# A second fold of the Fourier transform, along the sequence and along the channels, in an attention and Fourier-mix kernel

## The chip, the cores and the metric

The kernel runs on one core of one Trainium2 chip. The core has a matrix engine (TensorE, "PE" in the profile, with its weight loads as "PEld"), three engines for elementwise work (VectorE "DVE", ScalarE "ACT", GpSimd "POOL"), and a queue engine (SyncE, "SP") that here only issues DMAs. Matrix products land in PSUM[...]. The metric is the device time of one execution in microseconds (us). Every measurement is of the whole program.

## The reference

The program is talking-heads attention followed by an FNet block. Cut to what matters:

```python
# q, k, v: (8, 12, 448, 64); w_pre, w_post: (12, 12); all float32
scores = scale * (q @ k.transpose(0, 1, 3, 2))
scores = einsum('bhij,hg->bgij', scores, w_pre)       # mix the heads before softmax
attn = exp(scores - max(scores)); attn = attn / (sum(attn) + 1e-09)
attn = einsum('bhij,hg->bgij', attn, w_post)          # mix the heads after softmax
x = (attn @ v) as (8, 448, 768)                       # heads side by side
mixed = real(fft(fft(x, axis=1), axis=2))             # along 448 rows, then along 768 columns
u = x + mixed
un = (u - mean(u)) / sqrt(var(u) + 1e-06)
out = u + relu(un @ w_ch1) @ w_ch2                    # 768 -> 3072 -> 768
```

The Fourier transform is computed as products with tables of cosines and sines: the real part is a cosine product in both directions minus a sine product in both directions.

## The kernel before

Two phases follow each other. The **mix phase** (`mix_phase`) does attention and the Fourier transform for 8 batches; the **feed-forward phase** (`ffn_phase`) does the norm and the two big products. The change is in the first, apart from how the second reads its rows from DRAM.

**Steps of the mix phase.** A batch has 24 steps; there are 192 of them. One step T handles a set of query rows for all heads. Its chain runs over the engines: `emit_gather` (SyncE) brings scores of all heads together into `Kr`; `emit_premix` (TensorE, L425) mixes heads into the PSUM tile `mx`, of which there is one; `emit_max` (VectorE, L433) takes the row maximum; `emit_exp` (ScalarE, L441) writes the exponentials to `PP` and their sums to `den`; `emit_scale` makes the reciprocal on VectorE (L449, L450) and multiplies `PP` by it on **GpSimd** (L452, two instructions); `emit_postmix` (TensorE, L462) mixes heads again into `po`; `emit_turn` (VectorE, L473) transposes 32x32 blocks into `Pv`. The scaling of step T is emitted in loop step T-2 (`LM = 2`), its second mix in loop step T. So a loop step s holds the first mix of step s+2, then the second mix of step s, and then whatever is due.

**What is due** in a loop step comes from tables of step numbers: `AT_T` (transposes of q and k, L376), `AT_QK` (the score products, L399), `AT_AV` (products with v, L489), `AT_X` (transposes of the result to rows of x, L525), `AT_Z` (first stage of the Fourier transform, L570) and `AT_S` (its second stage, L584). Numbers above 24 reach into the steps of the next batch. On TensorE, VectorE and ScalarE the order of the program is the order in which these functions are called. On GpSimd and SyncE the framework's scheduler places the instructions[...].

**The rows and the folds.** The 448 rows of a batch are held as four groups `gi` of 112 or 113 rows (`X`): groups 1 and 3 are stored backward, so that row s of one tile meets row 448-s of the other. `fold` (GpSimd) is called when group 1 or 3 has been transposed. It makes, for the pair of groups, the sum and the difference of the two tiles (L547, two halves each), and from each the sum or difference of column d and column 768-d: `xe` (L551, L552) has 385 columns and `xo` (L557) 383. These six closures are put into the list `folds`, of which the loop takes one per step. In the queue of GpSimd they stand one behind the other: in a stretch of the queue that belongs to one batch the scheduler put all six between two scalings, once for the pair 0 and 1 and once for the pair 2 and 3.

**The two stages.** `emit_z` multiplies `xe` or `xo` (as the weights) with a table `ts` of 225 columns, for chunks of 96 to 128 columns of x: four chunks for the even part, three for the odd, each with two products, one per pair of groups, which accumulate. `emit_s2` multiplies the evacuated `z` with the tables `tce` or `tdo` of 385 columns: for each of two pairs four products for the even part and three for the odd. Its evacuation `done` adds the result to x in place on VectorE (L595, L597), and after the odd part sends the rows to the DRAM tensor of the batch, `u_scr[b]`: forward rows by DMAs from SyncE (L610, L612), backward rows by an indirect DMA from GpSimd (L604), which scatters them by a list of row numbers. The feed-forward phase loads them with `load_u` (L756).

Of the kernel before, what the change touches and what calls it, by code (L numbers as in the profile page):

```python
# [27 lines left out]

R = 5
# [9 lines left out]
PR = (GR, GR + 1)  # L39
XW = GR + 12  # L40
TOT = B * GS
# [10 lines left out]

SH = S // 2
DH = DM // 2
EVEN = [(0, 97), (97, 96), (193, 96), (289, 96)]
ODD = [(0, 128), (128, 128), (256, 127)]
# [6 lines left out]
AT_T = ((7, 0), (18, 18), (15, 17))  # L63
AT_QK = ((0, 2, 2), (0, 1, 2), (0, 1, 2), (0, 1, 2),
         (0, 1, 2), (1, 1, 2), (0, 1, 2), (0, 1, 2))
AT_AV = ((0, 2, 4), (0, 1, 4), (3, 4, 5), (2, 3, 4))
AT_X = (11, 20, 25, 29)
AT_Z = (38, 38, 38, 38, 42, 42, 42)
AT_S = ((41, 44), (49, 53))

ENG = {("tr", "q", 4): "d", ("tr", "q", 3): "a", ("tr", "k", 4): "a",
       ("tr", "k", 3): "d", "QK": "aa", "AV": "aa", "X": "aa", "z": "a"}
# [10 lines left out]
def _consts():  # L83
    s = np.arange(S)
    ang = 2.0 * np.pi * (np.outer(s, np.arange(SH + 1)) % S) / S
    ts = np.zeros((GR + 1, 2, 2, SH + 1))
    for n in range(2):
        for x, fn in enumerate((np.cos, np.sin)):
            ts[:PR[n], n, x] = fn(ang[n * GR:n * GR + PR[n]])
    d = np.arange(DH + 1)  # L90
    ang = 2.0 * np.pi * (np.outer(d, d) % DM) / DM
    tc = np.zeros((P, len(EVEN), DH + 1))
    for n, (d0, w) in enumerate(EVEN):
        tc[:w, n] = np.cos(ang[d0:d0 + w])
    td = np.zeros((P, len(ODD), DH + 1))
    for n, (d0, w) in enumerate(ODD):
        td[:w, n] = np.sin(ang[d0 + 1:d0 + 1 + w])
# [3 lines left out]
    for x in range(2):  # L101
        for r in range(R):
# [4 lines left out]
    at = S - GR * np.arange(2) - np.arange(GR)[:, None]  # L107
    return {"at": at.astype(np.uint32), "ts": ts.astype(np.float32),
            "tc": tc.astype(np.float32), "td": td.astype(np.float32),
            "mk": mk.astype(np.float32)}  # L110
# [142 lines left out]
def mix_phase(ctx, tc, ident, q, k, v, w_pre, w_post, u_scr, wts):  # L253
# [19 lines left out]
    pxf = pool("pxf", 2)  # L273
# [49 lines left out]
    rows = cst.tile([GR, 2], U32, name="rows")  # L323
    ts = cst.tile([GR + 1, 2, 2, SH + 1], F32, name="ts")
    tce = cst.tile([P, len(EVEN), DH + 1], F32, name="tce")
    tdo = cst.tile([P, len(ODD), DH + 1], F32, name="tdo")

    def emit_tables():
        for t, n in ((rows, "at"), (ts, "ts"), (tce, "tc"), (tdo, "td")):
            nc.sync.dma_start(out=t, in_=cn[n].ap())  # L330
        return []
# [660 lines left out]
```

## Time and profile before

| | us |
|---|---|
| median of 3 runs | 2513.55 (2512.15 to 2517.85) |
| the profiled execution, its own time | 2515.48 |
| its span | 2513.7 |
| TensorE busy in the span | 2412.0 (96%) |
| VectorE, ScalarE, GpSimd busy | 1498.9, 794.2, 636.0 |
| mix phase: first second mix to last one | 58.9 to 906.6 |
| TensorE busy between 200 and 800 us | 583.5 of 600 |
| VectorE, ScalarE, GpSimd busy, same stretch | 445.5, 387.2, 361.0 |

The span is the time from the first to the last instruction of the profiled execution. Busy times of different engines overlap. A row of the profile names the line, the engine, the operation, the tiles as output<-input, the shapes, and how often it ran; then its busy time and the mean time of one, and the idle time of the engine just before such instructions, with what ended it. A product of float32 shows as two records for each call in the program. "PEclk" is the share of the full clock that TensorE was granted.

### The profile page before, as it was taken

The page shows a single profiled execution, that of the slowest core. Times are in us where ns is not written, and L with a number is a line of the kernel's source. Part 1 is how long each engine was busy: PE and PEld are TensorE (multiplying, and loading weights), DVE is VectorE, ACT ScalarE, POOL GpSimd, SP SyncE. Part 2 cuts the span into 40 slices and gives each one's busy share as a digit, 9 for nine tenths or more (in the row PEclk, how much of TensorE's full clock was granted, in tenths as well). Part 3 has the DMA queues.
Part 4 walks back from the last instruction along what each step waited for, and adds up shares of the span by engine and source line. Part 5 has one row for each costly group of instructions (what it writes and reads, how often), then busy time and mean ns, then how long its engine had stood idle before and what let it go on. Part 6 is the DMA issues. An engine that isn't in the chain of part 4 may idle for free.

```text
span 2513.7 us, 47590 instructions
## 1 busy us (share of the span) xinstructions
PE 2412.0 (96%) x18544; PEld 1552.2 (62%) x18544; DVE 1498.9 (60%) x3103; ACT 794.2 (32%) x2084; POOL 636.0 (25%) x1001
## 2 busy tenths in 40 slices
PE   4899999999999986999999999999999999999999
PEld 2344444444444455767777777777777777777776
DVE  1777777777777645786466536653665466533333
ACT  2676666666666622223111101110111011111110
POOL 5475665657564431111010000000000000000000
PEclk8999999999999988999999999999999999999999
DMA  5454544555553448343634443444444444443331
GB/s 155 141 173 153 166 159 154 167 168 167 171 160 128 143 143 274 118 146 114 224 123 150 151 155 128 145 151 158 132 145 147 158 131 145 134 152 116 129 113 51
DMA packets 154911, 373.01 MB, mean 148 GB/s; under 512 B 22471, under 2 KB 75719, under 8 KB 154688
## 3 DMA queue, kind: packets, MB, share of 16 engines
q1 hardware_dynamic: 123360, 260.63, 30.6%
q0 software_dynamic: 31328, 109.34, 14.6%
q8 instruction: 148, 2.42, 0.4%
q14 instruction: 75, 0.61, 0.1%
HBM read 212.96 MB, written 74.34 MB: 114 GB/s over the span
## 4 chain that ended last, share of the span: by engine, by line
PE 85%; DMA 3%; POOL 3%; ACT 3%; DVE 3%; issue 1%; SPq 1%; ACTq 0%; POOLq 0%; DVEq 0%
PE psP L834 17%; PE psP L888 17%; PE psR L834 9%; PE psR L888 9%; PE mx L425 5%; PE ms L489 5%; PE psQ L888 4%; PE psQ L834 4%; PE po L462 4%; PE ms L399 4%; PE ms L584 3%; DVE nmx L433 2%; ACT PP L441 2%; PE ms L570 2%; DMA Kr<-Sb 2%; POOL xs L547 1%
## 5 line engine op out<-in xcount | busy, mean ns | idle before, releaser
L834 PE MATMUL psP<-ub,w1t 128*128 128x256 f32 x2016 | 462.9, 379 | 0.0
L888 PE MATMUL psP<-w2t,h 128*128 128x384 f32 x1344 | 460.9, 486 | 0.0
L834 PEld LDWEIGHTS psP<-ub,w1t 128*128 128x128 f32 x2016 | 382.9, 190 | 60.7
L888 PEld LDWEIGHTS psP<-w2t,h 128*128 128x128 f32 x1344 | 254.4, 190 | 165.9
L182 POOL DMA_DIRECT2D raw<-in_moe_w_ch_dram x120 | 69.9, 583 | 996.8 <-DVE tmp L221 965.2
L441 ACT ACTIVATE PP<-mx,nmx 128x448 f32<-128x448 f32 x384 | 239.9, 629 | 259.6 <-DVE nmx L433 225.5
L433 DVE TENSOR_REDUCE nmx<-mx 128x1 f32<-128x448 f32 x384 | 221.7, 619 | 165.5 <-PE mx L425 165.1
L452 POOL TENSOR_SCALAR PP<-PP,rcp 128x448 f32<-128x448 f32 x384 | 240.3, 637 | 287.8 <-DVE rcp L450 228.0
L894 DVE TENSOR_TENSOR u<-u,psP 128x384 f32<-128x384 f32 x336 | 183.4, 552 | 143.6 <-PE psP L888 141.4
L839 ACT COPY h<-psP 128x512 f32<-128x512 f32 x42 | 24.6, 585 | 761.7 <-PE psP L834 721.6
L834 PE MATMUL psR<-ub,w1t 128*128 128x256 f32 x1008 | 231.4, 379 | 0.0
L888 PE MATMUL psR<-w2t,h 128*128 128x384 f32 x672 | 230.5, 486 | 0.0
L425 PE MATMUL mx<-Kr,kw 60*64 60x448 f32 x1536 | 194.5, 551 | 31.0 <-ACT PP L441 18.1
L473 DVE STREAM_TRANSPOSE Pv<-po 128x896 f32<-128x896 f32 x192 | 212.3, 1106 | 9.8 <-PE po L462 9.7
L845 DVE TENSOR_TENSOR h<-h,psQ 128x512 f32<-128x512 f32 x42 | 28.9, 688 | 300.7 <-PE psQ L834 295.3
L834 PEld LDWEIGHTS psR<-ub,w1t 128*128 128x128 f32 x1008 | 191.4, 190 | 26.3 <-DVE ub L813 0.3
L462 PE MATMUL po<-PP,kw 60*32 60x448 f32 x3072 | 190.3, 552 | 13.7 <-POOL PP L452 9.9
L399 PE MATMUL ms<-kT,qT 64*60 64x448 f32 (+1 forms) x1536 | 187.8, 561 | 7.9 <-DVE kT L285 7.9
L285 ACT COPY Sb<-ms 124x448 f32<-124x448 f32 x384 | 184.1, 541 | 10.1 <-PE ms L399 6.8
L489 PEld LDWEIGHTS ms<-Pv,vv 64*64 64x64 f32 x5376 | 143.2, 133 | 69.0 <-issue 27.1
L888 PEld LDWEIGHTS psR<-w2t,h 128*128 128x128 f32 x672 | 127.2, 190 | 87.4
L489 PE MATMUL ms<-Pv,vv 64*64 64x120 f32 x5376 | 165.6, 268 | 0.0
(92 smaller groups left out, 2632.7 us busy)
## 6 DMA issues: line engine op xcount, KB each, us to landing
ub<-ub SPq DMA_DIRECT2D x294, 384.0 KB
Kr<-Sb SPq DMA_DIRECT2D x768, 105.0 KB
raw<-in_moe_w_ch_dram POOLq DMA_DIRECT2D x72, 256.0 KB, 3.2
raw<-in_moe_w_ch_dram POOLq DMA_DIRECT2D x48, 384.0 KB, 3.6
w<-wst POOLq DMA_DIRECT2D x18, 896.0 KB, 4.7
w<-wst POOLq DMA_DIRECT2D x12, 1344.0 KB, 5.8
w1t<-w SPq DMA_DIRECT2D x42, 384.0 KB
w2t<-w SPq DMA_DIRECT2D x42, 384.0 KB
```

The costliest lines, as they stand in the source:

```text
L285: (nc.scalar.copy if eng == "a" else nc.vector.tensor_copy)(out=out, in_=in_)
L399: nc.tensor.matmul(pss[x][64 * y:64 * y + r0 + 64 - lo, :S], st["qT", xx][64 * x:64 * x + 64, y, lo:r0 + 64], st["kT", xx][64 * x:64 * x + ...
L425: nc.tensor.matmul(mx[64 * z:64 * z + 64, x, :S], kw1[64 * x:64 * x + KR, :], Kr[64 * x:64 * x + KR, z, :], start=True, stop=True)
L433: nc.vector.tensor_reduce(nmx[:, x:x + 1], steps[T]["mx"][:, x, :S], axis=AX.X, op=ALU.max, negate=True)
L441: nc.scalar.activation(PP[:, x, :], steps[T]["mx"][:, x, :S], ACTF.Exp, bias=steps[T]["nmx"][:, x:x + 1], accum_out=den[:, x:x + 1])
L452: nc.gpsimd.tensor_scalar(PP[:, x, :], PP[:, x, :], rcp[:, x:x + 1], 1.0, op0=ALU.mult, op1=ALU.mult)
L462: nc.tensor.matmul(po[o:o + 32, z, :S], kw2[64 * z:64 * z + KR, y, :], PP[64 * z:64 * z + KR, :, c * HS:(c + 1) * HS], start=True, stop=True)
L473: nc.vector.transpose(g["Pv"][:, T % GT, :].rearrange("p (z s) -> p z s", z=2), steps[T]["po"][:, :, :S])
L489: nc.tensor.matmul(pss[y][64 * x:64 * x + 64, :nu * R], st["v", pr][64 * y:64 * y + 64, x, jb * D:(jb + 1) * D], _ap(Pv, 64 * y * rp + 32 ...
L834: nc.tensor.matmul(p[:, m, :], w1[i][:, kc, m * P:(m + 1) * P], ub[:, kc, :], start=i in OPENS and m == kc == 0, stop=kc == NK - 1, skip_g ...
L888: nc.tensor.matmul(p, lhs[i][:, kf, x * P:(x + 1) * P], w2[i][:, kf, :], start=i in OPENS and kf == 0, stop=kf == FM - 1, skip_group_check ...
L894: nc.vector.tensor_tensor(us_, us_, p, op=ALU.add)
```

## The change

The transform is folded a second time in both directions.

- `fold` keeps its six closures and, for the second pair of a batch, adds eight more. `both` takes the sum or the difference of the two pairs' `xe` (or `xo`), 385 or 383 columns; `again` takes from that the sums and the differences of columns n and w-1-n (192 or 191 columns each) and copies the middle one. The loop takes two closures per step in place of one.
- `emit_z` runs over four tiles of 97 columns or fewer in place of seven chunks. Each has four products with at most 113 columns of `ts`, none of which accumulates onto another, and each writes every second column of the PSUM tile.
- `emit_s2` has, for each pair and part, four products with 193 or 192 columns of a table `tcs`, again writing every second column.
- Groups 2 and 3 change their places: group 2 is now stored backward and group 3 forward (`PLACE`), all four have 113 rows, with a zero row where one is missing. Backward rows are scattered to DRAM tensors of their own, `u_rev`; `load_u` reads from both, so that a load is split where the source changes.
- The constant tables become smaller (`ts`, `tcs` in place of `ts`, `tce`, `tdo`).
- The tables of step numbers are new, and so are some places in the loop: the row maximum and the exponentials are called after the second mix and after the evacuations (`flush`); the scaling is called after the gather.

```diff
...
+PN = GR + 1
+PLACE = ((0, 1, (GR,)), (GR - 1, -1, (0, GR)), (GR, -1, ()), (1, 1, (0,)))
...
+ENDS = (GR, GR * 2 + 1, GR * 3 + 1, S)
...
-EVEN = [(0, 97), (97, 96), (193, 96), (289, 96)]
-ODD = [(0, 128), (128, 128), (256, 127)]
+DQ = DH // 2
+CW = DQ // 2 + 1
+FOLD = (((CW, CW - 1), (CW - 1, CW - 1)), ((CW - 1, CW - 1), (CW - 1, CW - 2)))
...
-AT_T = ((7, 0), (18, 18), (15, 17))
-AT_QK = ((0, 2, 2), (0, 1, 2), (0, 1, 2), (0, 1, 2),
-         (0, 1, 2), (1, 1, 2), (0, 1, 2), (0, 1, 2))
-AT_AV = ((0, 2, 4), (0, 1, 4), (3, 4, 5), (2, 3, 4))
-AT_X = (11, 20, 25, 29)
-AT_Z = (38, 38, 38, 38, 42, 42, 42)
-AT_S = ((41, 44), (49, 53))
-ENG = {("tr", "q", 4): "d", ("tr", "q", 3): "a", ("tr", "k", 4): "a",
-       ("tr", "k", 3): "d", "QK": "aa", "AV": "aa", "X": "aa", "z": "a"}
+AT_T = ((12, 10), (17, 16), (14, 18))
+AT_QK = ((1, 2, 2), (0, 1, 2), (0, 1, 2), (0, 1, 2),
+         (0, 1, 2), (0, 1, 2), (0, 1, 2), (0, 1, 2))
+AT_AV = ((0, 2, 3), (1, 3, 5), (3, 4, 5), (1, 2, 3))
+AT_X = (11, 20, 24, 29)
+AT_Z = (38, 38, 41, 41)
+AT_S = ((40, 44), (53, 55))
+ENG = {("tr", "q", 4): "d", ("tr", "q", 3): "a", ("tr", "k", 4): "d",
+       ("tr", "k", 3): "a", "QK": "aa", "AV": "aa", "X": "aa", "z": "a"}
...
-def mix_phase(ctx, tc, ident, q, k, v, w_pre, w_post, u_scr, wts):
+def mix_phase(ctx, tc, ident, q, k, v, w_pre, w_post, u_scr, u_rev, wts):
...
-    pxf = pool("pxf", 2)
+    pxf = pool("pxf")
...
-    rows = cst.tile([GR, 2], U32, name="rows")
-    ts = cst.tile([GR + 1, 2, 2, SH + 1], F32, name="ts")
-    tce = cst.tile([P, len(EVEN), DH + 1], F32, name="tce")
-    tdo = cst.tile([P, len(ODD), DH + 1], F32, name="tdo")
+    rows = cst.tile([PN, 2], U32, name="rows")
+    ts = cst.tile([PN, 2, 2, PN], F32, name="ts")
+    tcs = cst.tile([CW, 2, 2, 2, DQ + 1], F32, name="tcs")
...
-        for t, n in ((rows, "at"), (ts, "ts"), (tce, "tc"), (tdo, "td")):
+        for t, n in ((rows, "at"), (ts, "ts"), (tcs, "tc")):
...
-        back = g["gi"] % 2
+        first, sg, none = PLACE[g["gi"]]
...
-                o = MG + (GR - 1 - NB * e if back else NB * e)
-                sg = -1 if back else 1
+                o = MG + first + sg * NB * e
...
-            if y == 1 and pr == 2 and back:
-                o = MG if g["gi"] == 1 else MG + GR
-                nc.gpsimd.memset(XT[:, :, o:o + 1], 0.0)
+            if y == 1 and pr == 2:
+                for o in none:
+                    nc.gpsimd.memset(XT[:, :, MG + o:MG + o + 1], 0.0)
...
-        n = PR[g["gi"] // 2]
-        X = pxx.tile([GR + 1, DM], F32, name="X", tag="X")
+        X = pxx.tile([PN, DM], F32, name="X", tag="X")
...
+        st = batches[g["b"]]
...
-        n = PR[pair]
...
-        xe = pxf.tile([GR + 1, DH + 1], F32, name="xe", tag="xe")
-        xo = pxf.tile([GR + 1, DH - 1], F32, name="xo", tag="xo")
+        pl = nc.gpsimd
...
-                box.append(pxs.tile([GR + 1, DM], F32, name="xs", tag="xs"))
+                box.append(pxs.tile([PN, DM], F32, name="xs", tag="xs"))
...
-            nc.gpsimd.tensor_tensor(box[-1][:n, h], Xa[:n, h], Xb[:n, h], op=op)
+            pl.tensor_tensor(box[-1][:, h], Xa[:, h], Xb[:, h], op=op)
...
-            nc.gpsimd.tensor_copy(out=xe[:n, 0:DH + 1:DH], in_=xs[:n, 0:DH + 1:DH])
-            nc.gpsimd.tensor_tensor(xe[:n, 1:DH], xs[:n, 1:DH], xs[:n, DM - 1:DH:-1],
-                                    op=ALU.add)
+            xe = st["xe", pair] = pxf.tile([PN, DH + 1], F32, name="xe", tag=f"xe{pair}")
+            pl.tensor_copy(out=xe[:, 0:DH + 1:DH], in_=xs[:, 0:DH + 1:DH])
+            pl.tensor_tensor(xe[:, 1:DH], xs[:, 1:DH], xs[:, DM - 1:DH:-1], op=ALU.add)
...
-            nc.gpsimd.tensor_tensor(xo[:n, :], xd[:n, 1:DH], xd[:n, DM - 1:DH:-1],
-                                    op=ALU.subtract)
+            xo = st["xo", pair] = pxf.tile([PN, DH - 1], F32, name="xo", tag=f"xo{pair}")
+            pl.tensor_tensor(xo[:, :], xd[:, 1:DH], xd[:, DM - 1:DH:-1], op=ALU.subtract)
+        def both(par, op):
+            nm, w = ("xe", "xo")[par], DH + 1 - 2 * par
+            box.append(pxs.tile([PN, DM], F32, name="xs", tag="xs")[:, :w])
+            pl.tensor_tensor(box[-1], st[nm, 0][:, :], st[nm, 1][:, :], op=op)
+        def again(par, r):
+            if r == 0:
+                st["xf", par] = pxf.tile([PN, 2, 2, DQ + 1], F32, name="xf",
+                                         tag=f"xf{par}")
+            x, t = st["xf", par][:, r], box[-1]
+            n, w = DQ - par, DH + 1 - 2 * par
+            for y, op in enumerate((ALU.add, ALU.subtract)):
+                pl.tensor_tensor(x[:, y, :n], t[:, :n], t[:, w - 1:w - 1 - n:-1], op=op)
+            pl.tensor_copy(out=x[:, 0, n:n + 1], in_=t[:, n:n + 1])
...
-        batches[g["b"]]["xf", pair] = (xe, xo)
-    def emit_z(b, par, ch):
-        d0, w = (EVEN, ODD)[par][ch]
-        ps = ms_tile()
-        for pair, n in enumerate(PR):
-            nc.tensor.matmul(ps[:w, :SH + 1],
-                             batches[b]["xf", pair][par][:n, d0:d0 + w],
-                             ts[:n, pair, par, :], start=(pair == 0), stop=(pair == 1))
-        z = pzz.tile([w, SH + 1], F32, name=f"z{par}{ch}", tag=f"z{par}{ch}")
-        batches[b]["z", par, ch] = z
-        return [lambda: copy(ENG["z"], z[:, :], ps[:w, :SH + 1])]
+        if pair:
+            for par in range(2):
+                for r, op in enumerate((ALU.add, ALU.subtract)):
+                    folds.extend([lambda par=par, op=op: both(par, op),
+                                  lambda par=par, r=r: again(par, r)])
+    def emit_z(b, par, y):
+        w, at = FOLD[par][y]
+        ps = ms_tile().rearrange("p (n q) -> p n q", n=2)
+        for n, d0 in enumerate((0, at)):
+            for r in range(2):
+                k = GR if par ^ r else PN
+                nc.tensor.matmul(ps[:w, n, r:SH + 1:2],
+                                 batches[b]["xf", par][:k, par ^ r, y, d0:d0 + w],
+                                 ts[:k, par, r, :PN - r], start=True, stop=True)
+        z = pzz.tile([CW, 2, SH + 1], F32, name=f"z{par}{y}", tag=f"z{par}{y}")
+        batches[b]["z", par, y] = z
+        return [lambda: copy(ENG["z"], z[:w, :, :], ps[:w, :, :SH + 1])]
...
-        chunks, tab = ((EVEN, tce), (ODD, tdo))[par]
...
-        for ch, (_, w) in enumerate(chunks):
-            nc.tensor.matmul(ps[:n, :DH + 1], st["z", par, ch][:, i0:i0 + n],
-                             tab[:w, ch, :],
-                             start=(ch == 0), stop=(ch == len(chunks) - 1))
+        for y in range(2):
+            w, _ = FOLD[par][par ^ y]
+            for ch in range(2):
+                nc.tensor.matmul(ps[:n, y:DH + 1:2],
+                                 st["z", par, par ^ y][:w, ch, i0:i0 + n],
+                                 tcs[:w, par, y, ch, :DQ + 1 - y],
+                                 start=(ch == 0), stop=(ch == 1))
...
-                if back:
+                if pair ^ back:
...
-                        out=u_scr[b][:, :],
+                        out=u_rev[b][:, :],
...
-                            ap=rows[:GR, pair:pair + 1], axis=0),
-                        in_=X[:GR, :], in_offset=None)
-                    continue
-                nc.sync.dma_start(out=u_scr[b][i0:i0 + GR, :], in_=X[:GR, :])
-                if n > GR:
-                    nc.sync.dma_start(out=u_scr[b][i0 + GR:i0 + n, :], in_=X[GR:n, :])
+                            ap=rows[:n, pair:pair + 1], axis=0),
+                        in_=X[:n, :], in_offset=None)
+                else:
+                    nc.sync.dma_start(
+                        out=u_scr[b][pair * (SH + 1):pair * (SH + 1) + GR, :],
+                        in_=X[pair:pair + GR, :])
...
-        for at, par, ch in zip(AT_Z, [0] * len(EVEN) + [1] * len(ODD),
-                               [*range(len(EVEN)), *range(len(ODD))]):
-            due("full", f + at, lambda b=b, par=par, ch=ch: emit_z(b, par, ch))
+        for n, at in enumerate(AT_Z):
+            due("full", f + at, lambda b=b, n=n: emit_z(b, n // 2, n % 2))
...
-                emit_max(s + LM)
...
-            if 0 <= s + LM < TOT:
-                emit_exp(s + LM)
...
+            if 0 <= s + LM < TOT:
+                emit_max(s + LM)
+                emit_exp(s + LM)
...
-            if 0 <= s + LM < TOT:
-                emit_scale(s + LM)
-            if folds:
-                folds.pop(0)()
...
+            if 0 <= s + LM < TOT:
+                emit_scale(s + LM)
+            for _ in range(min(2, len(folds))):
+                folds.pop(0)()
...
-                n = min(P - p, S - r)
-                nc.sync.dma_start(out=us[t][p:p + n, x, :], in_=u_scr[b][r:r + n, :])
+                k = sum(r >= e for e in ENDS)
+                n = min(P - p, ENDS[k] - r)
+                src = (u_rev if k % 2 else u_scr)[b]
+                nc.sync.dma_start(out=us[t][p:p + n, x, :], in_=src[r:r + n, :])
...
+    u_rev = [scr.tile([S + 1, DM], F32, name=f"v_{b}") for b in range(B)]
...
-    mix_phase(tc, ident, q, k, v, w_pre, w_post, u_scr, wts)
-    ffn_phase(tc, ident, u_scr, wts, ub_scr, out.rearrange("b s d -> (b s) d"))
+    mix_phase(tc, ident, q, k, v, w_pre, w_post, u_scr, u_rev, wts)
+    ffn_phase(tc, ident, u_scr, u_rev, wts, ub_scr, out.rearrange("b s d -> (b s) d"))
```

## The prediction

> **What bounds the kernel now.** I read the busy times of the engines by stretch first, then the chain of waits, then the timeline at the places that the change touches. By stretch:
>
> ```profile
> core 0: us, PE busy (x) PEld busy (x) DVE busy (x) ACT busy (x) POOL busy (x), PEclk, DMA share, GB/s
> 200.00:800.00 600.00, 583.52 (x8528) 280.49 (x8522) 445.53 (x912) 387.22 (x1170) 361.04 (x563) 1.00 0.50 160
> ```
>
> In the steady part of the mix phase TensorE is busy 97% at full clock, the others 60 to 74%: what it is spared counts, unless something else then ends last. The chain of waits (start us, us, what) gives the price of each part of a step:
>
> ```profile
> 863.37 1.63 PE ms L489 x56
> 865.00 0.75 PE ms L399 x8
> 865.75 0.75 PE mx L425 x8
> 866.51 0.91 PE po L462 x16
> ```
>
> These four are a step with a score product and a product with v: 4.04 us. But a step has a floor, seen in the timeline of TensorE (start, duration of the merged piece, what, idle before and releaser):
>
> ```profile
> 402.99 0.93 PE L425 MATMUL mx<-Kr,kw 60*64 60x448 f32 x8
> 403.85 0.98 PE L462 MATMUL po<-PP,kw 60*32 60x448 f32 x16
> 404.76 0.98 PE L399 MATMUL ms<-kT,qT 64*64 64x448 f32 x8
> 405.67 0.98 PE L376 MATMUL ms<-ident,rawq 128*128 128x128 f32 x7
> 406.75 0.98 PE L425 MATMUL mx<-Kr,kw 60*64 60x448 f32 x8
> 408.29 0.99 PE L462 MATMUL po<-PP,kw 60*32 60x448 f32 x16 [0.56 <-POOL PP L452]
> ```
>
> From first mix to first mix it is 3.76 us, though the products are 0.75 + 0.91 + 0.75 + 0.95 = 3.36: the next first mix waits until the exponentials have emptied `mx`. The last line is the one I rest on: the second mix waits 0.56 us for GpSimd. Why, the timeline of GpSimd in the same place shows:
>
> ```profile
> 398.40 0.63 POOL L452 TENSOR_SCALAR PP<-PP,rcp 128x448 f32<-128x448 f32 x1
> 399.23 1.96 POOL L547 TENSOR_TENSOR xs<-X 113x384 f32<-113x384 f32 x2 [0.21 <-ACT X L285]
> 401.26 0.19 POOL L551 COPY xe<-xs 113x2 f32<-113x2 f32 x1
> 401.53 1.00 POOL L552 TENSOR_TENSOR xe<-xs 113x383 f32<-113x383 f32 x1
> 402.61 2.03 POOL L547 TENSOR_TENSOR xs<-X 113x384 f32<-113x384 f32 x2
> 404.72 1.00 POOL L557 TENSOR_TENSOR xo<-xs 113x383 f32<-113x383 f32 x1
> 405.88 1.05 POOL L604 DMA_INDIRECT u<-X,rows  x1 [0.16 <-issue]
> 406.98 2.48 POOL L452 TENSOR_SCALAR PP<-PP,rcp 128x448 f32<-128x448 f32 x4
> ```
>
> A whole fold, 6.5 us, and an indirect DMA stand between two scalings. A scaling is emitted two loop steps before the mix that needs it, so GpSimd may be about a step late for free; this block uses that up and 0.56 us more. GpSimd is 60% busy and yet at its limit here.
>
> Last, what an idle TensorE costs, at the end of the mix phase (columns as in the first fence):
>
> ```profile
> 904.00:912.00 8.00, 5.39 (x73) 3.39 (x74) 1.12 (x1) 0.53 (x3) 2.40 (x5) 0.58 0.14 43
> 912.00:920.00 8.00, 8.00 (x182) 6.47 (x180) 1.95 (x4) 2.54 (x11) 1.85 (x4) 0.99 0.29 98
> 926.40:932.60 6.20, 6.14 (x16) 4.54 (x17) 0.00 (x0) 1.38 (x4) 3.98 (x5) 0.50 0.78 265
> ```
>
> After some 3.5 us of idleness (903.0 to 906.6, and 923.2 to 926.5) it works at half clock for 5.5 to 6.1 us, which loses 2.7 to 3.0 us each time.
>
> [...]
>
> **The change part by part.**
>
> *Products.* The feed-forward rows price a record: L834 has 462.9 us for 2016 records of 256 columns (230 ns), L888 460.9 us for 1344 of 384 (343 ns), so 0.88 ns a column and about 4 ns. Before, a batch has 28 records of 385 columns in the second stage: the eight that start at 338.43 give way to the next line at 341.12, 336 ns each, 9.4 us together. The first stage has 28 of 225 columns, about 200 ns each: 5.6 us. After, it is 32 of 193 columns at 175 ns (5.6 us) and 32 of 113 columns at 119 ns (3.8 us; the formula says 104, the six transposes of 128 columns in the row of L525 take 137 with the start of a group). 15.0 becomes 9.4: 5.6 us less per batch. Weight loads of 97 or 113 columns (160 to 177 ns each) overlap one another as they do in L525, where the period is shorter than the load. Stepped writes I take at no extra cost; twice the cost would be 9.4 us per batch.
>
> *What the floor takes back.* I laid the due tables of both kernels over the prices, each step no shorter than 3.76 us. Before: 104.5 us per batch; with two folds' stalls 105.7. The trace has 108.9 (second mix of step 48 at 263.0, of step 168 at 807.3; a fifth of 544.3); the rest is spread over steps with evacuations and a few late gathers and I keep it. After: 100.1 without stalls. So 4.4 of the 5.6 us remain, as more steps end on the floor; one now has only a score product besides the mixes, 2.41 us of products under a floor of 3.76.
>
> *The second fold on GpSimd.* Building the changed kernel gives the order of its GpSimd queue. For each of the first seven batches, the first fold of the second pair and nearly all of the new closures stand between two neighbouring scalings, those of steps 7 and 8 of the next batch; the rest comes before the scaling of step 9. `both` is one operation of 385 elements, 1.06 us with the gap to its dependant. `again` is two of 192 elements and a copy. The nearest row below is L787, 4 elements in 0.27 us; between that and 1.00 us at 383, 192 elements are 0.63 us. Half of 1.00 is the lower bound (0.50), the full 1.00 the upper. I take 0.63[...]. So a pair is 1.06 + 2 x 0.70 + 0.26 = 2.7 us and the block 6.5 + 2.7 + 2.7 + about 2.5 = 14.4 us, where it was 6.5 plus the DMA's 1.05.
>
> *The stall.* Count from the first mix of the loop step that follows the transposes (398.89 in the fence). The scaling of step 7 ended at 0.1; as its own loop step is 0.6 us shorter, now at about 0.8. The block runs to 15.2, the scaling of step 8 to 16.5. TensorE has two loop steps (4.04 and 3.8) and a first mix (0.75): ready at 8.6. It waits 8.0 us. Nothing else can go ahead: [...]the products behind the second mix, with the next first mix, wait with it; VectorE's turn and ScalarE's exponentials then follow late. Against 0.6 now that is 7.4 us more per batch. The scaling of step 9 is 2.9 us behind and costs about 0.2. The other fold (groups 0 and 1) is as long as before, but its step is 0.6 us shorter: 0.6 more.
>
> *The clock.* Eight idle microseconds put TensorE to half clock: 2.5 us more (1 to 3[...]).
>
> *Sum per batch:* -4.4 + 7.4 + 0.6 + 2.5 = +6.1 us; seven batches: +43.
>
> *The end of the mix phase.* In the last batch no scaling is held up, but its first stage waits for all folds: the even part starts 12.9 us after x is there instead of 3.3, the odd one 18.2 instead of 6.4. Against that, x comes 4 us sooner as less is ahead of it, and the last products are shorter. I get +2 us. Tensors of their own spare the wait of SyncE for the indirect DMA (6.6 us once, at 940.7) and with it 2.4 us until the loads start at 948.1; the split loads (8 for 5 in the first block of rows, some 0.83 us each) give it back. Together +2.
>
> *Moved calls.* The maximum behind the evacuations is covered: VectorE has them done while the first mix (0.98 us) runs; only the four additions of the last second stage (2.2 us) could push it, and that falls into the stalled step. If that cover went, about 1 us per batch. The scaling's place in the loop moves nothing on TensorE. The smaller tables and the changed loads at the start: 0, within 3 either way. The feed-forward phase has the same work.
>
> **Sum:** 43 + 2 = +45 us on the span of 2513.7, which is by chance the median: **2558 us**.
>
> **Rivals.**
> *Faster:* the folds stay out of the way. Place and price: the block before the scaling of step 8. If the short operations were so cheap that the block took about 9 us instead of 14.4, stall and clock (3 + 1.5 us) would eat just the 4.4 us of products; below 7 us nothing is left but the gain, 7 x 4.4 - 2: 2485 us. For it: GpSimd is idle 40%, and TensorE bounds the phase. Against it: it would need 192 elements well under the 0.27 us that 4 elements take.
> *Milder:* the stall as computed, but little lost to the clock and short operations at 0.50: -4.4 + 6.6 + 0.6 + 0.5, seven times, +2: 2539 us.[...]
> *Heavier:* stepped PSUM writes at twice the price (+9.4 per batch, part of it under the floor): about 2620 us; or the short operations at 1.00 us: four or so before the scaling, +2.2 per batch and more behind it: about 2585. No row shows either.
> *It does not do what it says:* the products were halved but TensorE was not the bound; then no gain, and the stall stays: 2590. The 97% speak against it.
>
> **How the numbers follow.** As computed (2543 to 2580): 58%. Milder (2519 to 2543): 20%. Heavier: 11%. Block short enough to balance: 4%. Faster: 7%. The range 2519 to 2595 leaves out the faster and balanced cases and the far end of the heavier one, under 20%. 0.2% (5 us) is about what a measurement of this kernel can tell from no change; slower by more has 89%, within it 4%, faster 7%.
>
> **What would show it.** Right: once per batch, for seven batches, an idle stretch of TensorE of about 8 us before L462's counterpart, released by the scaling; the clock at half just after; the products of both stages at about 9.4 us per batch; `again` near 0.63 us an operation; steps otherwise at 3.8 to 5 us. Wrong: no such stretch, or a first mix that waits instead; products above 12 us per batch; a start of the feed-forward phase much later than 2 us relative to the last second mix.

## The result, and the profile after

The changed kernel takes 2659.11 us (2657.93 to 2661.93), the kernel before 2515.70 us beside it (2512.15 to 2519.99): a ratio of 1.057, 95% interval 1.055 to 1.059. The forecast of 2558 us, range 2519 to 2595, had the sign and missed the size: 143 us were lost, not 45.

The profiled execution has a span of 2659.5 us where it was 2513.7. I cut both spans at the first and at the last second mix (L462 before, L476 after):

| us | until the first second mix | first to last second mix | from there to the end |
|---|---|---|---|
| before | 58.9 | 847.7 | 1607.1 |
| after | 68.1 | 934.3 | 1657.1 |
| difference | +9.1 | +86.6 | +50.0 |
| forecast | 0, within 3 | +43 | +2 |

What ended last says where to look. This is the chain that ended last, by engine, of the kernel before:

```profile
PE 85%; DMA 3%; POOL 3%; ACT 3%; DVE 3%; issue 1%; SPq 1%; ACTq 0%; POOLq 0%; DVEq 0%
```

And of the kernel after, by engine and by line:

```profile
PE 71%; DMA 13%; POOL 7%; ACT 3%; DVE 2%; SPq 2%; issue 1%; ACTq 0%; POOLq 0%; DVEq 0%
PE psP L870 16%; PE psP L924 16%; PE psR L870 8%; PE psR L924 8%; DMA v<-X,rows 5%; PE mx L439 4%; PE psQ L870 4%; PE ms L503 4%; PE psQ L924 4%; DMA Kr<-Sb 4%; DMA u<-v 3%; PE po L476 3%; ACT PP L455 2%; PE ms L413 2%; POOL xs L557 2%; DVE nmx L447 2%
```

GpSimd rose by 4 points, the way the forecast had it. The 10 points by which transfers rose were in no step of the forecast. Three of them are named: the store by index (`v<-X,rows`), the gathers (`Kr<-Sb`), the loads of the feed-forward phase (`u<-v`).

**The stall that was forecast is there.** The timeline of GpSimd in the changed kernel at steps 7 and 8 of the fourth batch (start us, us, line, operation, tiles, count, idle time before and its releaser):

```profile
426.49 1.96 POOL L557 TENSOR_TENSOR xs<-X 113x384 f32<-113x384 f32 x2 [0.75 <-ACT X L300]
...
433.05 1.00 POOL L573 TENSOR_TENSOR xs<-xe 113x385 f32<-113x385 f32 x1
434.13 1.15 POOL L582 TENSOR_TENSOR xf<-xs 113x192 f32<-113x192 f32 x2
...
439.97 1.25 POOL L466 TENSOR_SCALAR PP<-PP,rcp 128x448 f32<-128x448 f32 x2
```

The timeline of TensorE in the same place:

```profile
434.43 0.98 PE L439 MATMUL mx<-Kr,kw 60*64 60x448 f32 x8
441.28 1.75 PE L476 MATMUL po<-PP,kw 60*32 60x448 f32 x16 [5.87 <-POOL PP L466]
442.96 2.44 PE L503 MATMUL ms<-Pv,vv 64*64 64x120 f32 x56
```

The block is 13.5 us long (14.4 forecast), TensorE waits 5.9 us for the scaling at its end (8.0 forecast), and its next pieces take 1.75 and 2.44 us where the price is 0.91 and 1.63. In all seven batches that have such a block the wait is 4.9 to 6.9 us. The slow pieces are the half clock, for which 2.5 us were set. In the view by stretch the column PEclk, behind the busy times, has 0.74 for the 7 us from 441 us, and the trace's own record of the clock has half of full speed from 437.8 to 444.6 us:

```profile
441.00:448.00 7.00, 6.72 (x112) 3.40 (x116) 2.62 (x6) 1.74 (x6) 6.63 (x10) 0.74 0.13 47
```

**A store by index that lands late was not forecast.** The view of its line, before (L604) and then after (L639):

```profile
L604 POOL DMA_INDIRECT u<-X,rows x16: 936/1042/1140, 256.4 to 951.1; - x16
...
DMA to landing us min/median/max: 3.4/3.6/8.3
```

```profile
L639 POOL DMA_INDIRECT v<-X,rows x16: 1002/1728/2559, 270.1 to 1042.3; - x16
...
ACT X L300: 34.8, 6
...
DMA to landing us min/median/max: 3.5/5.1/22.4
```

The first numbers are the duration on GpSimd, min, median and max in ns. Half of the stores, those of the second pair, now have 113 rows instead of 112. Those whose landing the trace has come after 18.7 to 22.4 us and hold GpSimd for 2.5 us instead of 1.0. ScalarE's copy into an X buffer of the ring waits for them, as the chain of waits goes on from the stall above:

```profile
445.26 22.34 DMA v<-X,rows
467.77 0.29 issue
468.06 0.48 ACT X L300
```

So steps 11 to 13 of this batch took 7.4, 9.4 and 4.2 us; the forecast had steps of 3.8 to 5. Copies stand in ScalarE's queue before exponentials, and TensorE's transposes of the next q and k (L390) wait for a PSUM buffer that such a copy frees (2.9 us in this batch).

**The loads of the feed-forward phase** and **the start** show the same kind of line. The chain of waits after the mix phase:

```profile
1049.95 20.56 DMA u<-v
1070.53 11.87 DMA u<-v
1082.48 1.03 DVE st L816 x2
```

and at the start:

```profile
30.93 25.94 DMA Kr<-Sb
56.91 2.24 PE mx L439 x5
```

The first gather needs 26 us. The constant tables, issued at 6.0 to 7.8 us, are the large transfers ahead of it on SyncE's queue; that they hold it back is tested below.

**Theory A, formed from this.** 113 rows in a store, 97 and 113 partitions in the tables, pieces of 97, 31, 47 or 17 rows in the loads have one thing in common: the counts are primes. The theory is that each of these transfers is late because of its count, whatever the rest of the kernel does, and that a count such as 112 or 128 would end the delay. Why a count should do that is not shown; that it goes with the way the packets run is. In the trace of the store, around one of 112 rows the software queue shows 48 packets of 6144 bytes and 16 of 3072, which is 112 rows; around one of 113 rows it shows 56 of 6144 and, new, 840 packets of 8 bytes, 15 times 56. Of the 56 packets of 6144 bytes of the store issued at 445.26 us never more than two are under way at once, and they take from 448.5 to 467.0 us. The 48 of the store of 112 rows issued at 391.96 us, up to 16 of them at once, take from 393.6 to 396.2 us. 112 is a multiple of 16, so the first two edits below take such counts, the third 128. **Theory B** is that only one of these matters and the others wait beside it, or that the late landings are a result of the stalls and of the second tensor, not of the row count.

### The profile page after: what moved, and what is told of

The parts are those of the page before. It is cut to its first block, busy times and chain, and to the rows that moved or that the text cites. A ratio compares the mean times of both kernels' runs of the same rounds, so it can differ in the third digit from the quotient of the medians.

```text
span 2659.5 us, 47850 instructions
## 1 busy us (share of the span) xinstructions
PE 2422.1 (91%) x18608; PEld 1558.9 (59%) x18608; DVE 1508.1 (57%) x3103; ACT 791.4 (30%) x2060; POOL 719.4 (27%) x1145
## 4 chain that ended last, share of the span: by engine, by line
PE 71%; DMA 13%; POOL 7%; ACT 3%; DVE 2%; SPq 2%; issue 1%; ACTq 0%; POOLq 0%; DVEq 0%
PE psP L870 16%; PE psP L924 16%; PE psR L870 8%; PE psR L924 8%; DMA v<-X,rows 5%; PE mx L439 4%; PE psQ L870 4%; PE ms L503 4%; PE psQ L924 4%; DMA Kr<-Sb 4%; DMA u<-v 3%; PE po L476 3%; ACT PP L455 2%; PE ms L413 2%; POOL xs L557 2%; DVE nmx L447 2%
## 5 line engine op out<-in xcount | busy, mean ns | idle before, releaser
L439 PE MATMUL mx<-Kr,kw 60*64 60x448 f32 x1536 | 222.6, 567 | 68.4 <-DMA Kr<-Sb 34.0
L476 PE MATMUL po<-PP,kw 60*32 60x448 f32 x3072 | 198.9, 576 | 47.8 <-POOL PP L466 45.2
L503 PEld LDWEIGHTS ms<-Pv,vv 64*64 64x64 f32 x5376 | 149.7, 137 | 75.5 <-issue 46.0
L503 PE MATMUL ms<-Pv,vv 64*64 64x120 f32 x5376 | 172.3, 275 | 0.2 <-issue 0.2
```

Of the source, the lines that this page charges most:

```text
L439: nc.tensor.matmul(mx[64 * z:64 * z + 64, x, :S], kw1[64 * x:64 * x + KR, :], Kr[64 * x:64 * x + KR, z, :], start=True, stop=True)
L476: nc.tensor.matmul(po[o:o + 32, z, :S], kw2[64 * z:64 * z + KR, y, :], PP[64 * z:64 * z + KR, :, c * HS:(c + 1) * HS], start=True, stop=True)
L503: nc.tensor.matmul(pss[y][64 * x:64 * x + 64, :nu * R], st["v", pr][64 * y:64 * y + 64, x, jb * D:(jb + 1) * D], _ap(Pv, 64 * y * rp + 32 ...
```

## The experiments

Where a table gives the three parts of the span, they are cut as above.

### The store, the loads and the tables, each alone in the changed kernel

First, 112 rows by index in both pairs; row 112 of the second goes by a plain DMA to the other tensor, from which it is loaded as a piece of one row.

```diff
-                            ap=rows[:n, pair:pair + 1], axis=0),
-                        in_=X[:n, :], in_offset=None)
+                            ap=rows[:GR, pair:pair + 1], axis=0),
+                        in_=X[:GR, :], in_offset=None)
+                    if n > GR:
+                        nc.sync.dma_start(out=u_scr[b][GR:n, :], in_=X[GR:n, :])
```

> Changed kernel, but the indirect store takes 112 rows instead of 113; row 112 of the second pair goes by a plain DMA of one row to the forward tensor. Theory A ([...]the store takes 22 us instead of 3.5, and the next transposed rows wait for the tile it still reads): the stores land in 3.5 to 5 us, the waits of ScalarE for them (34.8 us in six) go, steps 11 to 13 of a batch return to about 11.6 us, and 2659 becomes about 2596. Rival B (GpSimd, late from the second fold, is what steps 11 to 13 wait for, and the long store is hidden): within 10 us of 2659.

Second, loads cut at a multiple of 16 rows, the rest by itself.

```diff
+                n = n // 16 * 16 if n > 16 else n
                 src = (u_rev if k % 2 else u_scr)[b]
```

> Changed kernel, but each load of rows for the feed-forward phase is cut into a multiple of 16 rows and a rest of at most 15. Theory A ([...]one of them takes 20.6 us to land): the feed-forward phase starts 25 to 35 us sooner, 2659 becomes about 2630. Rival B (the loads are bound by the bytes, or by the time to issue them, of which there are now more): no gain, 2655 to 2670.

Third, the tables and the row numbers padded with zeros to 128 partitions.

```diff
...
-    ts = cst.tile([PN, 2, 2, PN], F32, name="ts")
-    tcs = cst.tile([CW, 2, 2, 2, DQ + 1], F32, name="tcs")
+    ts = cst.tile([P, 2, 2, PN], F32, name="ts")
+    tcs = cst.tile([P, 2, 2, 2, DQ + 1], F32, name="tcs")
```

> Changed kernel, but the constant tables and the row numbers are padded to 128 partitions. Theory A[...]: first second mix at 59 to 60 us instead of 68.0, 2659 becomes about 2650. Rival B (the later start comes from the new order of the first transposes and loads): 68 us and 2659 stay.

| us | time | start | mix | rest | ratio to before |
|---|---|---|---|---|---|
| after | 2659.1 | 68.1 | 934.3 | 1657.1 | 1.057 [1.055, 1.059] |
| store of 112 rows | 2651.6 | 67.4 | 887.4 | 1689.5 | 1.056 [1.054, 1.058] |
| loads cut | 2612.4 | 66.4 | 930.2 | 1610.2 | 1.040 [1.038, 1.042] |
| tables of 128 | 2632.7 | 43.3 | 933.8 | 1657.6 | 1.047 [1.045, 1.049] |

Each moves its own part; the loads and the tables gained 17 to 18 us more than was expected of them. The cut loads give back 47 us of the 50 that the feed-forward phase had lost, the tables 25 us of the start, more than the 9 us lost against before, whose `ts` also has 113 partitions. The chain of waits with tables of 128 has in place of the 25.94 us:

```profile
27.84 4.99 DMA Kr<-Sb
32.87 2.28 PE mx L441 x5
```

The packets of the tables show why. In the changed kernel those of `ts` (1808 bytes each) run from 9.1 to 25.8 us and those of `tcs` (6176 bytes) from 25.8 to 56.0 us, never more than two at once, and the gather lands behind them at 56.9. With 128 partitions both tables are there at 12.3 us, with up to 16 and 18 packets at once.

The store alone gained 7.5 us, which fits B in the total. But the mix phase lost 47 us and the rest rose by 32. My edit is the reason I hold likely: with row 112 in another tensor the pieces of 16 and of 80 rows become 1 and 15, and 1 and 79. The chain of waits of this kernel has, in the second block of rows as well as in the first:

```profile
995.39 19.81 DMA u<-u
...
1024.81 18.40 DMA u<-v
...
1117.28 21.68 DMA u<-v
```

Were that so, cutting the loads as well should keep all of the 47 us. The three together test it.

### The three together, and the order of the fold

> The changed kernel with the three repairs of row counts at once (stores by index of 112 rows, loads cut at multiples of 16 rows, tables padded to 128 partitions) and the order of the second fold left as it is. Theory A (three separate costs of transfers with an odd row count, each removed on its own ground, and under them the stall that was forecast): the first mix phase keeps the 47 us of the stores, the feed-forward phase the 47 us of the loads, the start the 25 us of the tables: 2659 - 119 = 2540 us, mix phase about 887 us, the rest about 1610 us, first second mix at 43 us. Theory B (one bottleneck, the DMA queue, of which each single repair has already shown most): the repairs overlap and the time stays above 2575 us. The forecast of 2558 us had left these costs out, so under A it should come within 20 us of this kernel.

2541.20 us (2538.12 to 2544.63), ratio 1.012 [1.010, 1.014]: A, to a microsecond of its 2540. Start 44.2, mix 887.5, rest 1605.6. The stores land after 3.5 to 5.6 us, 3.8 in the median, and what is left among the long waits of this kernel is the stall of the forecast (us in total, times, longest; weight loads and products of TensorE wait over the same time, so the two lines do not add up):

```profile
PEld po L479 <- POOL PP L469: 98.1, 73, 7.7
...
PE po L479 <- POOL PP L469: 45.8, 13, 6.9
```

So the row counts cost the changed kernel 118 us, and without them the forecast of 2558 is 17 us from the time. Not all of the 118 us belong to the 143 that were lost: the start is now 14.7 us shorter than that of the kernel before, whose `ts` has 113 partitions as well. These 14.7 us are also most of the 17. What the forecast did price stands at +39.8 us for the mix phase (43 forecast) and -1.5 for the rest (2 forecast). To see whether the stall costs what it seems to, I first fixed GpSimd's order in the program, so that at most two closures of a fold stand between two scalings, in the changed kernel as it is:

```diff
-    with tc.manual_schedule(engines={ET.PE, ET.DVE, ET.Activation}):
+    with tc.manual_schedule(engines={ET.PE, ET.DVE, ET.Activation, ET.Pool}):
```

> Changed kernel, but GpSimd too runs in the order of the program, so that at most two closures of the folds stand between two scalings. Theory A (the block of the second fold before one scaling costs 8 us of stall and some 2.5 us of half clock in each of seven batches): the wait of the second mix for the scaling falls from 150 us to under 30, the stretch of steps 7 and 8 from 15.7 to about 8 us, 2659 becomes about 2595. Rival B (GpSimd has too much to do over steps 5 to 12, in whatever order, so the wait only spreads over more steps): less than 25 us gained.

2658.36 us (2650.52 to 2665.99), mix phase 934.2 against 934.3: nothing, B. The stall itself went (steps 7 and 8 took 4.2 and 4.7 us in the mean of five batches), but the weight loads of the first mix waited 86.6 us for gathers where it had been 55.8. Then together with the three repairs:

> The same with the second fold's instructions also held to their place, two closures between one scaling and the next. Theory A (the stall of steps 7 and 8 is real and was hidden in the single repair only because the late stores held the same steps): 8 to 9.5 us less in each of seven batches, 2540 - 60 = 2475 to 2485 us, below the kernel before. Theory B (the fold's 7.6 us of added work on the scaling engine have to be done somewhere, and the steps that take them are as late): within 20 us of the kernel without this order.

2552.90 us (2549.93 to 2559.08), 12 us more than without the order; mix 899.2. So B again, and I had not foreseen by what. The timeline of GpSimd in step 4 of the fourth batch shows it:

```profile
399.01 2.14 POOL L362 DMA_DIRECT2D rawq<-in_q_dram  x3
403.32 0.70 POOL L362 DMA_DIRECT2D rawq<-in_q_dram  x1 [2.17 <-DMA vv<-in_v_dram]
404.01 0.13 POOL L528 MEMSET XT<- 128x6 f32 x1
404.10 1.25 POOL L469 TENSOR_SCALAR PP<-PP,rcp 128x448 f32<-128x448 f32 x2
```

Fixing GpSimd's order fixes its transfers too. Here a load of q waits 2.17 us for one of v, and the scaling that is written behind it waits with it; steps 3 to 5 take 6.6, 6.6 and 7.9 us in the mean of five batches, instead of 5.1, 4.5 and 5.4. Both runs say that this order is no better. They do not price the stall, since they took one away and made others.

### The same edits in the kernel before

Does the row count act without the rest of the change? The kernel before with 113 rows in the second pair's store, the extra row going to the spare row 448:

```diff
-    at = S - GR * np.arange(2) - np.arange(GR)[:, None]
+    at = S - GR * np.arange(2) - np.arange(GR + 1)[:, None]
+    at[GR] = S
...
-                        in_=X[:GR, :], in_offset=None)
+                        in_=X[:n, :], in_offset=None)
```

> The kernel before, its store by index of the second pair made 113 rows instead of 112 (the extra row goes to the spare row 448), nothing else. Theory A ([...]whatever the rest of the kernel does): the seven stores in the steady state land after 20 to 23 us instead of 3.5, the kernel gets slower by 20 to 47 us (2533 to 2560). Theory B (the slow landing belongs to the changed kernel, to its second tensor or to its order): they land in under 6 us and the time is within 5 us of 2512.

2585.04 us (2581.78 to 2587.03), ratio 1.029 [1.028, 1.031]: 73 us for one row, more than the 20 to 47 that A expected. In the profiles the mix phase has 63 of them, 910.9 us instead of 847.7. The line of the store:

```profile
L605 POOL DMA_INDIRECT u<-X,rows x16: 959/1728/2501, 257.8 to 1017.5; - x16
...
DMA to landing us min/median/max: 3.4/11.6/26.4
```

A holds: no second tensor, no new order, and the landing is the same 22 us. But another wait pays for it. In the chain of waits:

```profile
427.61 15.23 DMA Kr<-Sb
442.84 0.04 issue
442.88 0.98 PE mx L426 x2
```

The store was issued at 419 us and landed 22.4 us later, and a gather of Kr, issued in between, lands only when it is over. From 437 to 442 us only 12 packets of the gathers start, in the microsecond after 442 alone 37. Steps 9 and 10 of a batch took 4.5 to 10.3 and 6.3 to 8.8 us, where the kernel before has 4.3 and 4.2.

Then the loads alone: the kernel before, cut at the rows at which the changed kernel changes its tensor, but from one tensor.

```diff
-                n = min(P - p, S - r)
+                n = min(e for e in (GR, GR * 2 + 1, GR * 3 + 1, S) if e > r) - r
+                n = min(P - p, n)
```

> The kernel before, its loads of the feed-forward phase cut at rows 112, 225 and 337 of each batch as in the changed kernel, but from the one tensor; nothing else. Theory A ([...]the phase waits for them at its start): 40 to 50 us slower, 2552 to 2562 us, all of it after the last second mix. Theory B (it is the second tensor, or the late stores, that make the start of that phase late): within 6 us of 2512.

2566.30 us (2562.83 to 2569.94), ratio 1.020 [1.017, 1.022]: 51 us, just above the 40 to 50 of A. The span has 58.8, 851.1 and 1658.2 us: the last part is that of the changed kernel, 1657.1, and its chain of waits has the same two lines:

```profile
960.32 21.03 DMA u<-u
981.37 11.95 DMA u<-u
993.41 1.03 DVE st L781 x2
```

So neither the second tensor nor the late store delays that phase. The packets show the row counts directly. From 955.5 to 958.5 us and from 963 to 967 us, with loads of 97, 31 and 47 rows issued shortly before, one packet of 3072 bytes is under way at a time, where the kernel before has 11 to 18 from 948.5 to 955.5 us. After the load of 95 rows issued at 973.75 us five packets are under way from 975 to 977.5 us, after that of 111 rows issued at 981.37 us three from 985 to 988.5 us. Five divides 95 and three divides 111. So in packets at once these two counts lie between the primes and the loads of the kernel before. Last, the table, `ts` of 113 partitions padded to 128:

```diff
...
-    ts = cst.tile([GR + 1, 2, 2, SH + 1], F32, name="ts")
+    ts = cst.tile([P, 2, 2, SH + 1], F32, name="ts")
```

> The kernel before with its table of 113 partitions padded to 128. Theory A (the row count of the table holds the first gather back): the first second mix at 43 to 45 us instead of 58.9, and 12 to 16 us less, about 2499 us. Theory B (something else bounds the start): within 4 us of 2512.

2506.93 us (2500.89 to 2509.02), ratio 0.998 [0.997, 0.999]. The direction is A's, the size is not: the first second mix comes at 49.0 us instead of 58.9, not at 43 to 45, and 5 us come out, not 12 to 16. The first gather of its chain takes 7.25 us from 32.22, where the kernel before has 11.81 from 36.83. All of its tables are there at 17.0 us, so something else holds the start of this kernel as well; what, stays open.

### The second fold on VectorE

To price the stall, the second fold has to leave GpSimd. In the repaired kernel, `both` and `again` run on VectorE, in four lots of two closures at steps 9 to 12 (`later` is a list of its own beside `folds`):

```diff
-            pl.tensor_tensor(box[-1], st[nm, 0][:, :], st[nm, 1][:, :], op=op)
+            nc.vector.tensor_tensor(box[-1], st[nm, 0][:, :], st[nm, 1][:, :], op=op)
...
+            if later and s % GS in (9, 10, 11, 12):
+                for _ in range(2):
+                    later.pop(0)()
```

> The changed kernel with the three repairs of row counts and with the second fold (12 additions and subtractions, 4 copies of one column per batch) on VectorE, in four lots at steps 9 to 12 of the following batch; the first fold stays on GpSimd, whose block between the scalings of steps 7 and 8 is again the six operations of the kernel before. Theory A (the stall of steps 7 and 8 is the price of the second fold on the engine that scales, as forecast: 8 to 9 us in each of seven batches): steps 7 and 8 return to 4.5 and 3.3 us, the mix phase falls from 887 to about 825 to 835 us and the kernel takes 2541 - 57 = 2484 us, below the kernel before by some 28 us. Theory B (as in the run with the held order: work moved out of these steps is paid in the next): within 15 us of 2541.

2499.26 us (2498.66 to 2500.87), ratio 0.995 [0.993, 0.996]: faster than the kernel before by half a per cent, but 42 us were gained where A said 57. In the mean of five batches, steps 7 and 8 took 4.2 and 4.7 us, 7.8 less together. But steps 10 to 13 took 4.3, 5.1, 4.5 and 5.4, where the repaired kernel had 3.8, 3.8, 4.8 and 4.5: 2.3 of it paid back. The timeline of VectorE at the first lot shows why:

```profile
399.46 0.54 DVE L576 TENSOR_TENSOR xs<-xe 113x385 f32<-113x385 f32 x1
400.03 0.95 DVE L585 TENSOR_TENSOR xf<-xs 113x192 f32<-113x192 f32 x2
400.90 0.14 DVE L586 COPY xf<-xs 113x1 f32<-113x1 f32 x1
401.01 1.16 DVE L450 TENSOR_REDUCE nmx<-mx 128x1 f32<-128x448 f32 x2
```

VectorE has hardly a gap left in a short step (busy 7.27 of the 8 us from 398 to 406); a lot of 1.5 us stands before the row maximum, which the exponentials and the next first mix wait for. So one closure to a step, from step 9 to 16, into the longer steps:

```diff
-            if later and s % GS in (9, 10, 11, 12):
-                for _ in range(2):
-                    later.pop(0)()
+            if later and s % GS >= 9:
+                later.pop(0)()
```

> As the kernel with the second fold on VectorE, but its eight closures one to a step, steps 9 to 16, instead of two to a step. In the former, steps 10 to 13 took 5.1, 4.5, 5.4 and 5.2 us where they take 3.8, 3.8, 4.3 and 4.1 without the fold, about 4.5 us per batch. Theory A (VectorE has room in the long steps 14 to 16, where TensorE holds the time): half of the fold is hidden there, 2 us less in each of seven batches, 2499 - 14 = 2485 us. Theory B (VectorE is late wherever the fold stands): 2494 to 2504 us.

2493.81 us (2489.03 to 2495.87), ratio 0.991 [0.989, 0.994]. The span has 43.6, 841.3 and 1602.5 us. The profiled mix phase is 11 us shorter than with the lots, the median time 5 us, at the edge of the range that B gave. So the times don't settle this; the steps speak for A, and that expectation numbered the steps one too early and put their loss at 4.5 us instead of 2.3. Steps 10 to 13 now take 3.8, 4.2, 4.2 and 4.6 us, in sum 16.8 where the repaired kernel had 16.9, and 14 to 16 take 5.4, 4.1 and 5.0, as in the repaired kernel. This kernel is faster than both.

Waits for the scaling, which were 98.1 and 45.8 us, are down to one line among its long waits, the first below; the second is that of the kernel before:

```profile
PEld po L479 <- POOL PP L469: 48.1, 60, 2.0
PEld po L462 <- POOL PP L452: 45.4, 49, 2.4
```

From 887.5 us to 841.3 the mix phase lost 46 us, though VectorE has the fold's work now. As the steps that hold this work are no longer than without it, 46 us are about what the second fold cost on GpSimd.

## Why the prediction was wrong

**The step that failed** is the pricing of the transfers, in three places: one sentence for the tables ("the smaller tables and the changed loads at the start: 0, within 3 either way"), one term for the loads ("8 for 5 in the first block of rows, some 0.83 us each"), and a term that is missing. The store of the second pair gets a 113th row, and it was carried over at its price of before, in the block as its 1.05 us of issue and behind it as nothing. All three priced a transfer by its bytes or by its issue. The runs show in their place:

| term | forecast | in the change | where shown |
|---|---|---|---|
| store of 113 rows | 0 | +47 | mix phase 934.3 to 887.4 with 112 rows; in the kernel before 63 in the mix phase, 73 in all |
| pieces of the loads | +2.5 | +47 to +51 | rest 1657.1 to 1610.2 when cut; 51 in the kernel before |
| tables | 0, within 3 | +25; of these only 9 are lost against before, whose table has 113 partitions too | start 68.1 to 43.3 at 128 partitions |

The line "The feed-forward phase has the same work" was true of the engines and of no use. The sign that would have refuted the forecast was named, "a start of the feed-forward phase much later than 2 us relative to the last second mix", and it came.

**The stall** was right in place and cause and near in size, as the kernel with the three repairs lets one see without the rest. From the second mix of step 48 (254.4 us) to that of step 168 (827.0) a batch takes 114.5 us, where it took 108.9: 5.7 more, 6.1 forecast. Steps 7 and 8 take 16.7 us together, a mean of five batches, instead of 7.9: 8.8 more. The forecast had 7.4 for the stall and 2.5 for the clock; its wait was 2 us too long (5.9 measured, 8.0 forecast), of which 0.9 is the block, 13.5 us and not 14.4. The short operations took 0.61 us (192 columns) and 0.52 (191) where 0.63 was set for both. The other steps give 3.1 us less, where -4.4 and +0.6 were set. So the sum is closer than its parts: 1.1 us too much for the stall and its clock, 0.7 too much for the gain. The mix phase of that kernel lies 39.8 us above before, for a forecast of 43.

**The products** were cheap, nearly as assumed. The lines of the second stage and of the first in the changed kernel (busy us, mean ns):

```profile
L619 PE MATMUL ms<-tcs,z 96*113 96x192 f32 (+5 forms) x256 | 50.5, 341 | 0.6 <-ACT z L300 0.6
L604 PE MATMUL ms<-ts,xf 112*96 112x113 f32 (+5 forms) x256 | 30.5, 273 | 11.5 <-POOL xf L582 11.5
```

That is 6.3 us a batch where 5.6 was set, and 3.8 us, as set: 10.1 together, above the forecast of 9.4 and below the 12 that would have refuted it. The same measure gives 16.4 before, where the forecast had 15.0. So writing every second PSUM column costs nothing near the doubling of the heavier rival, which falls on that ground. How much of the 4.4 us per batch arrives is less clear: with the fold spread on VectorE a batch takes 107.3 us, only 1.6 less than before, and 1.0 of the rest stands at steps 7 and 8, which take 9.0 us instead of 7.9.

**The rivals.** "It does not do what it says" is weakened, not refuted. The kernel with the fold spread on VectorE is faster than before with the same products, but of the 26.4 us between the two profiled spans the start, with its padded tables, has 15.4, the mix phase 6.4 and the rest 4.6. "Faster" named the right lever (the block must shrink to leave the gain) but not the right obstacle.

**The range** reached to 2595 for slower stepped writes and short operations. It held no case of a transfer that lands late, though the change touches a store, the loads and the tables.

**What stays open.** That the data packets of a store of 113 rows run at most two at once is measured; what makes them do so is not shown, as the trace does not say which DMA engine moves a packet. Why the mix phase of the kernel before loses 63 us by the row that costs the changed one 47 is shown only as far as the waits differ (gathers here, X buffers as well there). The start of the kernel before is not explained beyond the 10 us that the padded table took.

## What to carry to other kernels

When an edit changes a row or partition count, look at the new count before its bytes: here one row more (112 to 113) in a store cost the kernel before 73 us, and padding the tables to 128 partitions, which adds bytes, took 25 us off the start of the changed one. A late transfer was paid for by what stood behind it on its queue (the first gather, 25.94 us behind the tables, 4.99 with tables of 128 partitions) or waited for its buffer (ScalarE's copies into X, 34.8 us in six waits), so price a store also by when it lands. And of work moved to another engine, ask what stands behind it there in the shortest steps: on GpSimd it was the scaling, on VectorE the row maximum.

## What the runs showed of the hardware that was not expected

- A store by index of 112 rows of 3072 bytes landed in 3.5 to 5.6 us in the mix phase, one of 113 rows in 21.5 to 23.3 us, with 2.4 to 2.6 us on GpSimd instead of 1.0 and 840 packets of 8 bytes beside its data. Its packets of 6144 bytes ran at most two at once, those of 112 rows up to 14 to 18 at once.
- Loads of 97, 31 and 47 rows ran one packet at a time, a load of 95 rows five, one of 111 rows three.
- Two-input operations of 113 x 385 elements took 1.00 us on GpSimd and 0.54 us on VectorE; of 113 x 192, 0.61 us on GpSimd. On VectorE those of 192 and 191 elements took 0.33 to 0.36 us in the kernel with one closure to a step; with two closures to a step 28 of 64 took 0.68 us or more, for a reason that stays open. One column less, 191, took 0.52 us on GpSimd.
- While such a store was under way a gather of 60 rows on the other queue needed 15.23 us.
